# Order of gathers and weight fetches in an expert layer behind block-sparse attention

## The chip, the core and the metric

The kernel runs on one core of a Trainium2 chip. The metric is the device time of one execution in microseconds (us). Five engines work side by side: TensorE (PE) multiplies matrices, VectorE (DVE) and ScalarE (ACT) do elementwise work and empty PE's accumulators, GpSimd (POOL) makes index patterns and here issues the indexed transfers, and SyncE (SP) issues the plain ones. Each engine takes its instructions in the order in which they stand in the program; semaphores hold one back until what it needs is there. A matrix product of f32 operands is two instructions on PE.

## The reference

Block-sparse attention on 4 batches of 8 heads, 768 positions and 64 features, then a layer of 8 experts in which every token goes to the one expert with the highest logit:

```python
scores = scale * np.matmul(q, k.transpose(0, 1, 3, 2))
scores = np.where(mask, scores, -1000000000.0)       # window, first and last blocks, 3 random blocks
scores = scores - np.max(scores, axis=-1, keepdims=True)
attn = np.exp(scores)
attn = attn / (np.sum(attn, axis=-1, keepdims=True) + 1e-09)
attn_out = np.matmul(attn, v)
x = attn_out.transpose(0, 2, 1, 3).reshape(B * S, H * D)     # 3072 tokens x 512
# experts
logits = x @ w_gate                                   # 3072 x 8
expert_idx = np.argmax(logits, axis=1)
gate_w = softmax(logits)[np.arange(N), expert_idx]    # shortened
for e in range(E):                                    # the tokens of expert e
    h = np.maximum(x_sorted[lo:hi] @ w1[e], 0.0)      # w1[e]: 512 x 1024
    y_sorted[lo:hi] = h @ w2[e]                       # w2[e]: 1024 x 512
return gate_w[:, None] * y                            # y put back in token order
```

All is float32. One expert's `w1` and its `w2` have 2048 KB each.

## The kernel before

The first part runs attention in 16 pairs of heads and writes the token rows, with the gate weight at their end, to a scratch tensor `x_d` in device memory. The second part sorts the tokens by expert into tiles of 128 tokens, 28 with these inputs, and for each tile gathers its rows, transposes them, runs both layers and scatters the result into the output. The first five tiles (`KA = 5`) are laid out early, from the first three batches alone, so that their gathers and weights can start during attention (routing table "A"); the others use table "B", which is ready only after attention.

The start. `kT` and `qT` of the first pair are transposed by PE and copied half by VectorE, half by ScalarE:

```python
def turn(b, pr, which, first=None):
    ...
    for half in range(2):
        tp = ps_t.tile(...)[:] if first is None else first[:, half, :CW]
        for c in range(HC):
            nc.tensor.transpose(tp[:, c * P : (c + 1) * P], src[...], ident[:])
        if half == 0:
            nc.vector.tensor_copy(dst[:, :CW], tp)
        else:
            nc.scalar.copy(dst[:, CW:], tp)
        yield
```

Constants for the token layout, called in step 30 of the 96 steps of attention. `sm` is a pool with a place of its own for every tile; `small` has four buffers per tag, which are passed on in turn:

```python
def route_consts():
    iota("first_w", ...); iota("thr", ...); iota("kx", ...); iota("iota_r", ...)
    t1 = sm.tile([P, B, NCH], I32, name="t1")
    nc.gpsimd.iota(t1[:], pattern=[[S, B], [1, NCH]], base=1, channel_multiplier=NCH)
    t2 = sm.tile([P, 2, NT], I32, name="t2")
    flat = t1.rearrange("p b c -> p (b c)")
    nc.vector.tensor_scalar(t2[:, 0, :], flat, scalar1=6, ..., op0=ALU.arith_shift_right)
    nc.vector.tensor_scalar(t2[:, 1, :], flat, scalar1=63, ..., op0=ALU.bitwise_and)
    tok = rt["tok"] = sm.tile([P, 2, NT], BF16, name="tok")
    nc.gpsimd.tensor_copy(tok[:], t2[:])
    ...                                   # lt, all, zero, keep: GpSimd memsets
def rows_out(n, half):                    # end of each half pair of attention
    ...
    lg = small.tile([P, HC, 2, E], F32, name="lg")
```

The parts of a tile. There are four buffers for gathered rows, two each for `w1`, `w2` and the transposed rows:

```python
def gather(i):
    xg = st[i]["xg"] = keep_xg[i % 4]
    nc.gpsimd.indirect_dma_start(out=xg[:], in_=x_d[: N - S, :] if i < KA else x_d[:, :],
                                 in_offset=bass.IndirectOffsetOnAxis(ap=of("g", i, P), axis=0), ...)
def fetch(i, layer):
    e = nc.sync.value_load(of("xe", i, 1), ...)           # the tile's expert
    if layer == 1:
        w = st[i]["w1"] = keep_w1[i % 2];  nc.sync.dma_start(w[:], w1v[:, bass.ds(e, 1)]...)   # L606
    else:
        w = st[i]["w2"] = keep_w2[i % 2];  nc.sync.dma_start(w[:], w2v[:, bass.ds(e, 1)]...)   # L609
def turn_x(i):
    ...                                                   # 4 transposes on PE (L614), one copy
def layer1(i, *between):
    hT = st[i]["hT"] = xp.tile([P, FB, P], F32, name="hT")
    for g in range(2):
        hp = upper["ps_h"].tile(...)
        ...                                               # 16 products into hp (L630)
        ...                                               # relu into hT, VectorE or ScalarE
        if g == 0:
            for do in between:
                do()
def layer2(i, group):
    zp = ps_o.tile([P, DM], F32, name="zp", tag="o")
    ...                                                   # 8 products into zp (L645)
    zo = xp.tile([P, DM], F32, name="zo")
    ...                                                   # zo = zp * gate weight, which lies in xg
    nc.gpsimd.indirect_dma_start(out=out[:, :], ..., in_=zo[:], ...)      # the scatter (L654)
```

The order of the parts. GpSimd and PE keep the order of the program until `by_hand.close()`; the other engines, and those two afterwards, are ordered by a scheduler. The tiles above 24 are in one of the branches of a switch, by how many there are:

```python
            if (n, half) == (NA + 2, 0):                  # in attention, table A
                tokens("A", TA, KA)
                for i_ in range(2):
                    gather(i_)
                    fetch(i_, 1)
                    fetch(i_, 2)
    ...
    layer1(0, lambda: rows_out(*steps[-1][:2]), lambda: turn_x(1))
    for i in range(NT):                                   # NT = 24
        if i == 0:
            ranks("B", TA, NT)
        for t in {1: (3, 4), 2: ()}.get(i, (i + 2,)):
            if t != KA:
                gather(t)
        fetch(i + 2, 1)
        if i + 1 < NT:
            layer1(i + 1, lambda: turn_x(i + 2))
        if i == 0:
            count("B"); layout_b()
        if i == 1:
            tokens("B", NT, NB_)
        layer2(i, "rows_out")
        fetch(i + 2, 2)
        if i == 1:
            gather(KA)
        if i == 2:
            judge()
        if i == KA + 1:
            by_hand.close()
    for extra in tc.Switch(...):
        last = NT + extra
        for i in range(NT, last):
            if i + 2 < last:
                gather(i + 2)
            layer1(i, *([lambda: turn_x(i + 1)] if i + 1 < last else []))
            if i + 2 < last:
                fetch(i + 2, 1)
            layer2(i, "rows_out")
            if i + 2 < last:
                fetch(i + 2, 2)
```

So on PE the first layer of tile i+1 comes ahead of the second layer of tile i, and the transpose of tile i+2 stands in the middle of that first layer. Fetches into a buffer wait until the products that read it are done.

Of the kernel before, what the change touches and what calls it, by code (L numbers as in the profile page):

```python
# [9 lines left out]
I32 = mybir.dt.int32  # L10
# [7 lines left out]
def kernel(  # L18
# [12 lines left out]
    P = 128  # L31
    B, H, S, D = q.shape
# [3 lines left out]
    NCH = S // P  # L36
# [7 lines left out]
    NT = N // P  # L44
    NC = NT + E - 1
    TA = NT - NCH
    KA = 5
# [136 lines left out]
    sm = ctx.enter_context(tc.tile_pool(name="sm", bufs=1))  # L184
    work = ctx.enter_context(tc.tile_pool(name="work", bufs=2))
    small = ctx.enter_context(tc.tile_pool(name="small", bufs=4))
# [199 lines left out]
    def route_consts():  # L386
        iota("first_w", [P, E], [[-1, E]], E, 0)
        iota("thr", [P, NT], [[P, NT]], 0, 0)
        iota("kx", [1, NC], [[1, NC]], 0, 0)
        iota("iota_r", [P, P], [[1, P]], 0, 0)  # L390

        t1 = sm.tile([P, B, NCH], I32, name="t1")
        nc.gpsimd.iota(t1[:], pattern=[[S, B], [1, NCH]], base=1, channel_multiplier=NCH)
        t2 = sm.tile([P, 2, NT], I32, name="t2")
        flat = t1.rearrange("p b c -> p (b c)")
        nc.vector.tensor_scalar(t2[:, 0, :], flat, scalar1=6, scalar2=None, op0=ALU.arith_shift_right)
        nc.vector.tensor_scalar(t2[:, 1, :], flat, scalar1=63, scalar2=None, op0=ALU.bitwise_and)
        tok = rt["tok"] = sm.tile([P, 2, NT], BF16, name="tok")
        nc.gpsimd.tensor_copy(tok[:], t2[:])
        lt = rt["lt"] = sm.tile([P, P], BF16, name="lt")  # L400
        nc.gpsimd.memset(lt[:], 1.0)
        nc.gpsimd.affine_select(
            out=lt[:], in_=lt[:], compare_op=ALU.is_gt, fill=0.0, base=0, pattern=[[1, P]], channel_multiplier=-1,
        )
        rt["all"] = sm.tile([P, P], BF16, name="all_")
        nc.gpsimd.memset(rt["all"][:], 1.0)
        rt["zero"] = sm.tile([P, E], F32, name="zero")
        nc.gpsimd.memset(rt["zero"][:], 0.0)
        keep = rt["keep"] = sm.tile([P, E, TA], F32, name="keep")
        nc.gpsimd.memset(keep[:], 1.0)  # L410
        nc.gpsimd.memset(keep[:, :, 0:1], 0.0)
# [154 lines left out]
    def tokens(ph, T, n):  # L566

        tp = ps_x.tile([P, 2, n], F32, name="tok" + ph, tag="xr")
        for t in range(T):
            nc.tensor.matmul(tp[:], lhsT=rt["or" + ph][:, t, :], rhs=rt["tk" + ph][:, t], start=(t == 0), stop=(t == T - 1))  # L570
        lo = sm.tile([P, n], F32, name="lo" + ph)
        nc.vector.tensor_scalar_add(lo[:], tp[:, 1, :], -1.0)
        tv = sm.tile([P, n], F32, name="tv" + ph)
        nc.vector.scalar_tensor_tensor(tv[:], in0=tp[:, 0, :], scalar=64.0, in1=lo[:], op0=ALU.mult, op1=ALU.add)
        g = rt["g" + ph] = sm.tile([P, n], I32, name="g" + ph)
        nc.vector.tensor_scalar(g[:], tv[:], scalar1=0.0, scalar2=float(T * P - 1), op0=ALU.max, op1=ALU.min)
        none = sm.tile([P, n], F32, name="none" + ph)
        nc.vector.tensor_scalar(none[:], tv[:], scalar1=0.0, scalar2=float(2 * N), op0=ALU.is_lt, op1=ALU.mult)
        s_ = rt["s" + ph] = sm.tile([P, n], I32, name="s" + ph)
        nc.vector.tensor_add(s_[:], tv[:], none[:])  # L580
# [14 lines left out]
    def gather(i):  # L595
        xg = st[i]["xg"] = keep_xg[i % 4]
        nc.gpsimd.indirect_dma_start(  # L597
            out=xg[:], out_offset=None, in_=x_d[: N - S, :] if i < KA else x_d[:, :], in_offset=bass.IndirectOffsetOnAxis(ap=of("g", i, P), axis=0),
        )

    def fetch(i, layer):

        e = nc.sync.value_load(of("xe", i, 1), min_val=0, max_val=E - 1)
        if layer == 1:
            w = st[i]["w1"] = keep_w1[i % 2]
            nc.sync.dma_start(w[:], w1v[:, bass.ds(e, 1)].rearrange("p e c f -> p (e c) f"))  # L606
        else:
            w = st[i]["w2"] = keep_w2[i % 2]
            nc.sync.dma_start(w[:], w2v[:, bass.ds(e, 1)].rearrange("p e a d -> p (e a) d"))  # L609

    def turn_x(i):
        tp = ps_t.tile([P, DB, P], F32, name="tp0", tag="t") if i == 0 else upper["ps_m"].tile([P, DB, P], F32, name="tpg")
        for c in range(DB):
            nc.tensor.transpose(tp[:, c, :], st[i]["xg"][:, c * P : (c + 1) * P], ident[:])  # L614
        st[i]["xT"] = keep_xT[i % 2]

        if i <= KA:
            nc.scalar.copy(st[i]["xT"][:], tp[:])
        else:
            nc.vector.tensor_copy(st[i]["xT"][:], tp[:])  # L620
# [5 lines that stand above are left out]
            hp = upper["ps_h"].tile([P, FB // 2, P], F32, name="hp")  # L626
            for m in range(FB // 2):
                fb = g * (FB // 2) + m
                for c in range(DB):
                    nc.tensor.matmul(  # L630
                        hp[:, m, :], lhsT=st[i]["w1"][:, c, fb * P : (fb + 1) * P], rhs=st[i]["xT"][:, c, :],
                        start=(c == 0), stop=(c == DB - 1),
                    )
            if g == 0 and i >= KA:
                nc.vector.tensor_relu(hT[:, : FB // 2, :], hp[:])  # L635
            else:
                nc.scalar.activation(hT[:, g * (FB // 2) : (g + 1) * (FB // 2), :], hp[:], AF.Relu)  # L637
# [3 lines that stand above are left out]
# [31 lines left out]
    for i in range(len(steps) + 1):  # L672
        at = steps[i] if i < len(steps) else None
        if at is not None:
            n, half, g = at
            if half == 1 and g == 0 and n + 2 < len(pairs):
                load(*pairs[n + 2])
            for c in range(g * GR, (g + 1) * GR):
                scores(n, half, c)
            if i == 1:  # L680
                make_mix()
            if i == 30:
                route_consts()
        if i > 0:
            n, half, g = steps[i - 1]
            for c in range(g * GR, (g + 1) * GR):
                attend(n, half, c)

        if at is not None and at[2] == 1:
            n, half, _ = at  # L690
            turning = turn(*pairs[n + 1], half) if n + 1 < len(pairs) else iter(())
            next(turning, None)
            if i > 3:
                rows_out(*steps[i - 2][:2])
            for _ in turning:
                pass

            if (n, half) == (NA, 0):
                ranks("A", 0, TA)
            if (n, half) == (NA, 1):  # L700
                count("A")
                layout_a()
            if (n, half) == (NA + 2, 0):
                tokens("A", TA, KA)
                for i_ in range(2):
                    gather(i_)
                    fetch(i_, 1)
                    fetch(i_, 2)
            if n + 1 == len(pairs) and half == 1:
                turn_x(0)  # L710
    lend(lent, ps_h=2, ps_m=2)
    layer1(0, lambda: rows_out(*steps[-1][:2]), lambda: turn_x(1))
    for i in range(NT):
        if i == 0:
            ranks("B", TA, NT)
        for t in {1: (3, 4), 2: ()}.get(i, (i + 2,)):
            if t != KA:
                gather(t)
        fetch(i + 2, 1)
        if i + 1 < NT:  # L720
            layer1(i + 1, lambda: turn_x(i + 2))
        if i == 0:
            count("B")
            layout_b()
        if i == 1:
            tokens("B", NT, NB_)
        layer2(i, "rows_out")
        fetch(i + 2, 2)
        if i == 1:
            gather(KA)  # L730
        if i == 2:
            judge()
        if i == KA + 1:
            by_hand.close()

    for extra in tc.Switch(nc.values_load(rt["more"][0:1, 0:1], min_val=0, max_val=NC - NT), NC - NT + 1):
        last = NT + extra
        for i in range(NT, last):
            if i + 2 < last:
                gather(i + 2)  # L740
            layer1(i, *([lambda: turn_x(i + 1)] if i + 1 < last else []))
            if i + 2 < last:
                fetch(i + 2, 1)
# [3 lines that stand above are left out]
# [54 lines left out]
```

## Time and profile before

| | |
|---|---|
| time, median of 3 runs | 904.13 us (900.5 to 904.48) |
| span of the profiled execution | 904.3 us |
| PE busy | 833.7 us, 92% of the span |
| DVE, ACT, POOL busy | 293.9, 214.9, 68.2 us |
| device memory read, written | 143.79 MB, 13.73 MB |
| PE clock, mean | 0.971 of full |

The page first gives each engine's busy time, then the span in 40 slices of about 22.6 us with a digit for the busy tenths, and then groups of like instructions. A row of a group names the line of the kernel, the engine, the operation, the tile written and the tiles read, shape, type and count; after the bar stand busy us and the mean ns of one, and then how long the engine sat idle just ahead of these instructions and what ended most of that. A timeline row has the start, the length, the engine (SPq is SyncE issuing a transfer), the line, and in brackets the idle time before it with what ended it. The name `w` stands for both layers' weights; L630 is the first layer, L645 the second. Attention reaches to about 424 us, the expert part from there to about 890.

### The profile page before, as it was taken

How to read it: one execution, taken by the hardware profiler on the slowest of the kernel's cores; microseconds unless marked ns; L12 is line 12 of the kernel's file. 1: busy time of each engine (PE TensorE's matmuls, PEld its weight loads, DVE VectorE, ACT ScalarE, POOL GpSimd, SP SyncE). 2: the span in 40 equal slices, each digit the busy share in tenths (PEclk: the TensorE clock that was granted, in tenths of full speed). 3: DMA queues.
4: the chain of work that ended last, by engine and by line, in shares of the span. 5: the costliest groups of instructions: out<-in, count | busy, mean ns of one | idle time of the engine just before them, and what ended most of it. 6: DMA issues, size and time to landing. Idle time of an engine off the chain costs nothing.

```text
span 904.3 us, 12472 instructions
## 1 busy us (share of the span) xinstructions
PE 833.7 (92%) x5104; PEld 529.0 (59%) x5104; DVE 293.9 (33%) x613; ACT 214.9 (24%) x306; POOL 68.2 (8%) x102
## 2 busy tenths in 40 slices
PE   6999999999999998999969777998999999999993
PEld 3455545555455554556857555766576766766671
DVE  4455555555555567554600000011111101111110
ACT  2444454444544444443111000000000000000000
POOL 4000000000000000010010001010110101010100
PEclk7999999999999999999989888999999999999997
DMA  7122222212222237410359755579788797879950
GB/s 157 44 64 68 55 71 71 71 42 64 71 53 70 54 72 257 183 39 20 123 214 335 274 194 190 192 277 341 267 308 306 266 353 272 321 272 350 397 180 9
DMA packets 119238, 157.52 MB, mean 174 GB/s; under 512 B 56435, under 2 KB 72819, under 8 KB 119156
## 3 DMA queue, kind: packets, MB, share of 16 engines
q1 hardware_dynamic: 112544, 142.32, 47.3%
q0 software_dynamic: 4480, 13.75, 4.0%
q8 instruction: 44, 0.72, 0.3%
q10 hardware_dynamic: 2132, 0.41, 0.2%
q14 instruction: 38, 0.31, 0.1%
HBM read 143.79 MB, written 13.73 MB: 174 GB/s over the span
## 4 chain that ended last, share of the span: by engine, by line
PE 48%; issue 38%; DMA 7%; POOL 3%; DVE 2%; another core or an unknown queue 0%; ACTq 0%; POOLq 0%; ACT 0%; DVEq 0%
PE s L216 15%; PE op L236 15%; DMA out_dram<-zo,sB 5%; PE xr L252 4%; PE s L219 3%; PE hp L630 3%; PE xr L257 3%; PE tp L197 3%; POOL xg L597 2%; PE zp L645 2%; POOL out_dram L654 1%; DMA xg<-x_rows,gB 1%; DVE esum L227 1%; DMA wg<-in_moe_w_gate_dram 1%; DVE orA L561 0%
## 5 line engine op out<-in xcount | busy, mean ns | idle before, releaser
L630 PE MATMUL hp<-xgT,w 128*128 128x128 f32 x1792 | 218.9, 283 | 16.0 <-DMA w<-in_moe_w_dram 15.9
L630 PEld LDWEIGHTS hp<-xgT,w 128*128 128x128 f32 x1792 | 214.6, 199 | 32.3 <-issue 19.0
L645 PE MATMUL zp<-w,hT 128*128 128x512 f32 x448 | 197.0, 593 | 0.6 <-DVE hT L635 0.6
L221 ACT ACTIVATE e<-s 128x768 f32<-128x768 f32 x192 | 155.8, 813 | 94.2 <-PE s L219 92.3
L216 PE MATMUL s<-qT,kT 64*128 64x384 f32 x768 | 166.9, 513 | 0.0
L227 DVE TENSOR_TENSOR esum<-esum,e 128x768 f32<-128x768 f32 x128 | 122.6, 958 | 69.9 <-ACT e L221 63.2
L236 PE MATMUL op<-e,v_sb 128*64 128x384 f32 x768 | 144.8, 499 | 0.0
L645 PEld LDWEIGHTS zp<-w,hT 128*128 128x128 f32 x448 | 83.0, 190 | 95.0 <-issue 94.2
L637 ACT ACTIVATE hT<-hp 128x512 f32<-128x512 f32 x33 | 19.7, 597 | 389.7 <-PE hp L630 386.8
L216 PEld LDWEIGHTS s<-qT,kT 64*128 64x128 f32 x768 | 63.8, 188 | 64.9 <-ACT e L221 37.6
L236 PEld LDWEIGHTS op<-e,v_sb 128*64 128x64 f32 x768 | 46.7, 136 | 80.1 <-issue 79.9
L653 DVE TENSOR_SCALAR zo<-zp,xg 128x512 f32<-128x512 f32 x23 | 17.3, 751 | 217.8 <-PE zp L645 217.8
L219 PE MATMUL s<-pen,oh 64*128 64x384 bf16 x384 | 63.6, 325 | 0.0
L635 DVE TENSOR_SCALAR hT<-hp 128x512 f32<-128x512 f32 x23 | 15.9, 692 | 118.1 <-PE hp L630 111.4
L227 DVE TENSOR_TENSOR esum<-e 128x768 f32<-128x768 f32 x32 | 30.7, 959 | 64.8 <-ACT e L221 64.8
L654 POOL DMA_INDIRECT out_dram<-zo,sB x23 | 23.2, 1009 | 304.3 <-DVE zo L653 304.3
L252 PEld LDWEIGHTS xr<-ones,esum 128*128 128x128 f32 x384 | 45.4, 192 | 1.2 <-DVE esum L227 1.2
L252 PE MATMUL xr<-ones,esum 128*128 128x1 f32 x384 | 44.9, 244 | 0.0
L614 PE MATMUL tpg<-ident,xg 128*128 128x128 f32 x108 | 18.3, 296 | 26.8 <-DMA xg<-x_rows,gB 19.6
L597 POOL DMA_INDIRECT xg<-x_rows,gA x5 | 6.4, 1284 | 370.1 <-PE s L219 368.9
L219 PEld LDWEIGHTS <-oh 64*128 64x128 bf16 x384 | 19.4, 95 | 25.1 <-issue 0.6
L257 PE MATMUL xr<-mix,oT 128*128 128x144 f32 x192 | 31.4, 300 | 0.0
(185 smaller groups left out, 307.8 us busy)
## 6 DMA issues: line engine op xcount, KB each, us to landing
w<-in_moe_w_dram SPq DMA_DIRECT2D x56, 2048.0 KB, 12.0
k_sb<-in_k_dram SPq DMA_DIRECT2D x32, 192.0 KB, 3.6
v_sb<-in_v_dram SPq DMA_DIRECT2D x16, 384.0 KB, 3.2
x_rows<-xb SPq DMA_DIRECT2D x16, 384.0 KB, 3.8
q_sb<-in_q_dram SPq DMA_DIRECT2D x30, 192.0 KB, 3.3
q_sb<-in_q_dram ACTq DMA_DIRECT2D x2, 192.0 KB, 4.9
xg<-x_rows,gB POOLq DMA_INDIRECT x23, 7.7
out_dram<-zo,sB POOLq DMA_INDIRECT x23, 7.8
```

The costliest lines, as they stand in the source:

```text
L197: nc.tensor.transpose(tp[:, c * P : (c + 1) * P], src[:, half * HC + c].rearrange("p h d -> p (h d)"), ident[:],)
L216: nc.tensor.matmul(s[:, hh, :CW], lhsT=kT[r, c * P : (c + 1) * P], rhs=qT[r, cols], start=True, stop=False)
L219: nc.tensor.matmul(s[:, hh, :CW], lhsT=oh[r, c, :], rhs=pen[r, cols], start=False, stop=True)
L221: nc.scalar.activation(e[:], s[:, :, :CW], AF.Exp, scale=scale)
L227: nc.vector.tensor_add(t[:], es[(n, half, 0)][:] if c == 1 else t[:], e[:])
L236: nc.tensor.matmul(op[hh * D : (hh + 1) * D, :], lhsT=v_sb[:, hh, c, :], rhs=e[:, hh, :], start=(c == 0), stop=(c == NCH - 1),)
L252: nc.tensor.matmul(xr[:, HC * M + 2 * m + hh : HC * M + 2 * m + hh + 1], lhsT=esum[:, hh, m * P : (m + 1) * P], rhs=ones[:], start=True, s ...
L257: nc.tensor.matmul(xr[:, m * M : (m + 1) * M], lhsT=oT[:, m * P : (m + 1) * P], rhs=mix[:, pr, :], start=True, stop=True)
L597: nc.gpsimd.indirect_dma_start(out=xg[:], out_offset=None, in_=x_d[: N - S, :] if i < KA else x_d[:, :], in_offset=bass.IndirectOffsetOnAx ...
L630: nc.tensor.matmul(hp[:, m, :], lhsT=st[i]["w1"][:, c, fb * P : (fb + 1) * P], rhs=st[i]["xT"][:, c, :], start=(c == 0), stop=(c == DB - 1),)
L645: nc.tensor.matmul(zp[:], lhsT=st[i]["hT"][:, fb, :], rhs=st[i]["w2"][:, fb, :], start=(fb == 0), stop=(fb == FB - 1),)
L654: ins = nc.gpsimd.indirect_dma_start(out=out[:, :], out_offset=bass.IndirectOffsetOnAxis(ap=of("s", i, P), axis=0), in_=zo[:], in_offset=N ...
```

## The change

Gathers are issued three tiles ahead of the tile in work instead of two, which the four row buffers allow; three, not two, are issued in attention. The fetch of first-layer weights moves behind the first layer of the tile before last, whose buffer it takes, so that it no longer goes out together with a second-layer fetch. The two integer tiles of the layout constants take buffers of the logit tiles instead of places of their own, which also moves their two VectorE operations to the place in the attention where they are called.

```diff
-        t1 = sm.tile([P, B, NCH], I32, name="t1")
+        t1 = small.tile([P, B, NCH], I32, name="t1", tag="lg")
         nc.gpsimd.iota(t1[:], pattern=[[S, B], [1, NCH]], base=1, channel_multiplier=NCH)
-        t2 = sm.tile([P, 2, NT], I32, name="t2")
+        t2 = small.tile([P, 2, NT], I32, name="t2", tag="lg")
...
                 tokens("A", TA, KA)
+                for i_ in range(3):
+                    gather(i_)
                 for i_ in range(2):
-                    gather(i_)
                     fetch(i_, 1)
                     fetch(i_, 2)
...
     layer1(0, lambda: rows_out(*steps[-1][:2]), lambda: turn_x(1))
+    fetch(2, 1)
     for i in range(NT):
         if i == 0:
             ranks("B", TA, NT)
-        for t in {1: (3, 4), 2: ()}.get(i, (i + 2,)):
-            if t != KA:
-                gather(t)
-        fetch(i + 2, 1)
+        gather(i + 3)
         if i + 1 < NT:
             layer1(i + 1, lambda: turn_x(i + 2))
+            fetch(i + 3, 1)
...
         layer2(i, "rows_out")
         fetch(i + 2, 2)
-        if i == 1:
-            gather(KA)
         if i == 2:
             judge()
...
         for i in range(NT, last):
-            if i + 2 < last:
-                gather(i + 2)
+            if i + 3 < last:
+                gather(i + 3)
```

## Prediction

> **What bounds the kernel now.** I read the page's 40 slices first. TensorE (PE) has digit 9 nearly everywhere, so the attention stage, up to about 424 us, leaves nothing to a change of order. It falls to 6 to 7 in slices 21 to 25, at a reduced clock. The costliest groups name what it waits for:
>
> ```profile
> L630 PE MATMUL hp<-xgT,w 128*128 128x128 f32 x1792 | 218.9, 283 | 16.0 <-DMA w<-in_moe_w_dram 15.9
> L645 PE MATMUL zp<-w,hT 128*128 128x512 f32 x448 | 197.0, 593 | 0.6 <-DVE hT L635 0.6
> L614 PE MATMUL tpg<-ident,xg 128*128 128x128 f32 x108 | 18.3, 296 | 26.8 <-DMA xg<-x_rows,gB 19.6
> ```
>
> The expert stage waits 15.9 us for weights ahead of the first layer and 26.8 us for gathered tokens ahead of the transpose, and never for second-layer weights. The windows of the attention stage, the early expert stage and the late one show what this does to PE busy time (second column), clock, DMA share and GB/s (last three):
>
> ```profile
> 100.00:200.00 100.00, 100.00 (x665) 52.90 (x664) 54.16 (x107) 46.73 (x65) 0.00 (x0) 1.00 0.26 64
> 448.00:592.00 144.00, 114.55 (x616) 85.81 (x615) 13.89 (x24) 10.95 (x18) 15.60 (x15) 0.89 0.65 231
> 592.00:817.00 225.00, 211.68 (x1238) 154.71 (x1239) 29.90 (x45) 8.36 (x14) 29.84 (x30) 1.00 0.83 299
> ```
>
> PE's timeline shows a gather wait, GpSimd's timeline (POOL) why it is there:
>
> ```profile
> 505.50 3.73 PE L630 MATMUL hp<-xgT,w 128*128 128x128 f32 x32
> 515.64 1.12 PE L614 MATMUL tpg<-ident,xg 128*128 128x128 f32 x4 [6.40 <-DMA xg<-x_rows,gB]
> 516.55 5.74 PE L630 MATMUL hp<-xgT,w 128*128 128x128 f32 x32
> 522.13 7.03 PE L645 MATMUL zp<-w,hT 128*128 128x512 f32 x16
> ```
> ```profile
> 506.72 1.01 POOL L654 DMA_INDIRECT out_dram<-zo,sA  x1 [17.32 <-ACT zo L651]
> 508.03 1.00 POOL L597 DMA_INDIRECT xg<-x_rows,gB  x1 [0.30 <-issue]
> ```
>
> GpSimd works in order. The gather of tile 6 stands behind the output scatter of tile 3, which waits for tile 3's second layer (done at 505.5). The transpose wants tile 6 half a first layer later, at 509.1; the gather, issued at 508.03, lands after 7.6 us. The first layer's second half then takes 5.74 us, not the usual 3.74: the clock has dropped. SyncE's timeline shows both weight fetches going out as a pair:
>
> ```profile
> 607.26 0.37 SPq L609 DMA_DIRECT2D w<-in_moe_w_dram  x1
> 607.82 0.45 SPq L606 DMA_DIRECT2D w<-in_moe_w_dram  x1
> ```
>
> The first-layer weights of the pair are needed one tile later, and PE starts on them at 624.66, 16.84 us after the issue.
>
> At the very start VectorE (DVE) waits 4.6 us for a layout constant, with the copy that the scores need queued behind it:
>
> ```profile
> 13.64 0.16 POOL L393 IOTA t<- 128x24 int32 x1
> 13.84 0.18 DVE L396 TENSOR_SCALAR t<-t 128x24 int32<-128x24 int32 x1 [4.64 <-POOL t L393]
> ...
> 14.01 0.55 DVE L201 COPY qT<-first 128x384 f32<-128x384 f32 x1
> ...
> 14.61 0.50 PEld L197 LDWEIGHTS first<-ident,q_sb 128*128 128x128 f32 x3 [4.22 <-DVE qT L201]
> ```
>
> **What the Trainium skill says.** "TensorE: Matmul & The Clock Gate", Part 1, says that an idle window of about 3.4 us halves PE's clock and that it takes about one busy window to restore it. The trace agrees: mean clock 0.89 where the gather waits lie, and 5.74 against 3.74 us above. So a removed wait gives back more than itself. "DMA: Bandwidth & Descriptors", section "Issuing engines are not separate DMA queues", says that transfers from all issuers share the same 16 engines and interleave. The trace agrees: a gather lands after 3.6 us at the least, 7.7 in the median, with the weights beside it. The same page's "Rules for kernel authors" advises issuing a transfer early and waiting for it late, which is what this change does.
>
> **Part 1, gathers three ahead.** An undisturbed tile takes 14.45 us (the first layer starts at 846.74 and the next at 861.19): half a first layer 3.57, transpose 0.43, other half 3.58, second layer 6.87. The four gather waits, with the slow matmuls after them, as the timeline has them against this:
> - tile 3: transpose at 459.61, due at 452.24, so 7.37; transpose and half layer take 5.54 for 4.01, so 1.53 more. Sum 8.90.
> - tile 6: 6.57 + 2.48 = 9.05. Tile 7: 6.69 + 2.61 = 9.30. Tile 8: 6.85 + 2.60 = 9.45.
>
> Together 36.7 us. In the new GpSimd order the gather of tile 3 goes out with tiles 0 to 2, near 389 us, into a fourth buffer nobody has used. Each later gather, of tile i+3, stands behind the scatter of tile i-1, about 2.5 us after that tile's second layer ends. Its transpose is then one first layer (7.58), one second layer (6.87) and half a first layer (3.57) away: 18.0 us, or 15.5 after the issue. The longest gather of the trace took 8.9. The gathers cost the same; they add nothing to PE. I count all 36.7. From tile 9 on, the old kernel's scheduler already had its gathers this far ahead (two follow each other at 555.34 and 556.63), so nothing more is to be had there.
>
> **Part 2, first-layer fetches behind the first layer.** The weight waits: between the first-layer starts at 576.65 and 810.14 lie 15 tiles, 233.49 us, against 15 x 14.45 = 216.75, so 16.74. One more at 487.3: 2.08 of waiting and a half layer of 5.27 for 3.57, so 3.78. Together 20.5. Now w1 of tile i+3 is issued when the first layer of tile i+1 ends, instead of after the second layer of tile i. It is due two second layers and a first one later: 6.87 + 7.58 + 6.87 = 21.3 us, against some 13.9 before. The slowest weight fetch took 16.7 us as half of a pair, one alone 8.3. The second-layer fetch keeps its place and its 22.0 us.
>
> Throughput allows it: two fetches of 2048 KB (4.19 MB), a gather (128 x 520 x 4 = 0.27) and a scatter (0.26) are 4.72 MB in 14.45 us, 327 GB/s. The steady stage above averages 299, but only because the DMA stands idle between pairs; where it is full it moves more:
>
> ```profile
> 601.30:602.30 1.00, 1.00 (x3) 0.38 (x2) 0.00 (x0) 0.00 (x0) 0.00 (x0) 1.00 1.01 412
> 606.30:607.30 1.00, 1.00 (x4) 0.28 (x3) 0.03 (x1) 0.00 (x0) 0.00 (x0) 1.00 0.01 4
> 831.40:861.20 29.80, 29.23 (x170) 21.33 (x169) 4.08 (x6) 1.20 (x2) 3.99 (x4) 1.00 1.04 401
> ```
>
> The last row is the tail, whose code already fetches in the alternating way: 401 GB/s and PE busy for 29.23 of 29.80 us. I count all 20.5.
>
> **Part 3, constants late.** Moved into the rotating buffers of the logit tiles, the two VectorE operations leave the start and stand after about a third of the attention. The copy of qT could then begin when PE has done its transposes, 9.94 + 0.85 = 10.79, instead of 14.01: 3.2 us, all on the path, since PE is busy from there on. PE runs at half clock around there; if the rise to full clock doesn't move along, only half of the 3.2 stays. Later VectorE waits once for GpSimd's following constants, about 1.4 us (GpSimd's row from tok to keep in the start), while it is idle nearly half the time; I charge 0.5.
>
> **Sum.** 36.7 + 20.5 + 3.2 - 0.5 = 59.9 us; 904.1 - 59.9 = 844.2. I predict 844 us. Not touched: the 0.57 us wait at the entry of the tail, and the 14.5 us from PE's last second layer (889.7) to the end.
>
> **Rivals.**
> - *The DMA becomes the bound.* If the streams sustained only the 299 GB/s of the steady stage, a tile would take 4.72 / 299 = 15.8 us and part 2 would vanish, perhaps with new waits for second-layer weights: about 865. Against it stand 401 GB/s in the tail and the idle microseconds between pairs.
> - *The gather stays late behind the scatter.* It is still behind it in GpSimd's queue. If it missed its transpose again, part 1 would shrink to tile 3: about 872. Against it: 15.5 us of room for 8.9.
> - *A new wait in order.* SyncE now interleaves 1 to 3 loads of expert numbers (about 0.57 us each) with the fetches, and gathers 5 and up need the second routing table. VectorE finishes that table's inputs at 453.28, 11.4 us after its counts at 441.91; PE now comes to it after 14.6. Were it late, a few us are lost once: about 847.
>
> **Range and chances.** The first two rivals I give about 5% each, partial forms included. The runs before spread by 4 us, the start is good for 1.6 to 3.5, and small waits I don't see may keep 3 to 6 us. The range is 839 to 852. Faster by over 2% (under 886) 0.97, within 2% 0.025, slower 0.005.
>
> **What would show it.** Right: no PE wait for xg; waits for w before L630 near zero; first layers every 14.45 us through the whole stage; granted clock 1.00 after about 19 us; GB/s steady near 327 in the late expert stage; the first scores near 12.3 us instead of 15.44; PE ending near 830. Wrong: a wait for w before L645, a period near 15.8, or an xg wait still behind the scatter.

## The result, and the profile after

| | before | changed |
|---|---|---|
| time, median of 4 runs each | 904.31 us | 845.94 us (845.3 to 846.65) |
| span of the profiled execution | 904.3 us | 844.9 us |
| PE busy, share of the span | 833.7 us, 92% | 820.4 us, 97% |
| mean PE clock | 0.971 | 0.993 |

The changed kernel takes 0.936 of the time before, 95% interval 0.933 to 0.939. Predicted were 844 us, with a range of 839 to 852.

The mean clock of the changed kernel is a little too high: its record has no half clock from 0 to 20 us, although the products there run at half speed until 17.4 us (four score products take 1.49 us at 16.02 and 0.81 at 17.51). For the start, the lengths of the products are the better measure.

The rows of the page's group list for the first and the second layer, in the changed kernel:

```profile
L630 PE MATMUL hp<-xgT,w 128*128 128x128 f32 x1792 | 209.1, 275 | 0.0
L645 PE MATMUL zp<-w,hT 128*128 128x512 f32 x448 | 197.0, 593 | 0.9 <-DVE hT L635 0.9
```

Ahead of the first layer 16.0 us of waiting have become 0.0, and the mean of one product has gone from 283 to 275 ns, because the clock no longer falls in this stage (1.00 in the windows below). The transpose has left the page's list; the view of its tile shows all 108 products between 272 and 273 ns and no idle time of PE:

```profile
L614 PE MATMUL tpg<-ident,xg x108: 272/273/273, 427.6 to 806.0; 128*128 128x128 f32 x108
```

The windows of the expert stage (PE busy in the second column; clock, DMA share and GB/s at the end) show PE busy for every microsecond of them:

```profile
443.00:580.00 137.00, 137.00 (x815) 100.34 (x814) 20.03 (x42) 12.04 (x20) 20.19 (x20) 1.00 0.90 320
580.00:770.00 190.00, 190.00 (x1082) 137.63 (x1081) 26.53 (x39) 7.76 (x13) 26.77 (x27) 1.00 0.92 325
```

Why the gather is no longer late is seen when GpSimd's timeline is laid beside PE's:

```profile
506.27 1.02 POOL L654 DMA_INDIRECT out_dram<-zo,sA  x1 [12.15 <-ACT zo L651]
507.59 0.98 POOL L597 DMA_INDIRECT xg<-x_rows,gB  x1 [0.30 <-issue]
```
```profile
505.05 3.73 PE L630 MATMUL hp<-xgT,w 128*128 128x128 f32 x32
508.62 0.60 PE L614 MATMUL tpg<-ident,xg 128*128 128x128 f32 x4
509.06 3.74 PE L630 MATMUL hp<-xgT,w 128*128 128x128 f32 x32
512.63 7.03 PE L645 MATMUL zp<-w,hT 128*128 128x512 f32 x16
519.50 3.73 PE L630 MATMUL hp<-xgT,w 128*128 128x128 f32 x32
523.07 0.60 PE L614 MATMUL tpg<-ident,xg 128*128 128x128 f32 x4
```

The gather still stands right behind a scatter and goes out 2.5 us after a second layer has ended (505.05). But it is for the transpose at 523.07, not for the one at 508.62, and has 15.5 us. First layers follow each other at 14.45 us (505.05, 519.50). SyncE's timeline no longer has pairs; L609 fetches second-layer weights, L606 first-layer ones:

```profile
606.39 0.37 SPq L609 DMA_DIRECT2D w<-in_moe_w_dram  x1
613.98 0.37 SPq L606 DMA_DIRECT2D w<-in_moe_w_dram  x1
```

The view of the weight tiles gives 7.9, 9.7 and 13.3 us from issue to landing (least, median, most), against 8.3, 12.0 and 16.7 before. At the start, VectorE waits for nothing but PE's transposes before it copies qT, at 11.21 instead of 14.01 us:

```profile
10.33 0.85 PE L197 MATMUL first<-ident,q_sb 128*128 128x128 f32 x3
...
11.21 0.56 DVE L201 COPY qT<-first 128x384 f32<-128x384 f32 x1 [1.64 <-PE first L197]
...
11.83 0.90 PE L197 MATMUL first<-ident,q_sb 128*128 128x128 f32 x3 [0.65 <-DVE qT L201]
...
12.66 1.65 PE L216 MATMUL s<-qT,kT 64*128 64x384 f32 x4
```

The first scores start at 12.66 instead of 15.44 us.

### The profile page after: what moved, and what is told of

Its sections match the earlier page's. It is cut to its first block, busy times and chain, and to the rows that moved or that the text cites. A ratio compares the mean times of both kernels' runs of the same rounds, so it can differ in the third digit from the quotient of the medians.

```text
span 844.9 us, 12494 instructions
## 1 busy us (share of the span) xinstructions
PE 820.4 (97%) x5104; PEld 519.8 (62%) x5104; DVE 293.4 (35%) x613; ACT 214.6 (25%) x306; POOL 69.3 (8%) x102
## 4 chain that ended last, share of the span: by engine, by line
issue 44%; PE 42%; DMA 5%; POOL 4%; DVE 3%; another core or an unknown queue 0%; POOLq 0%; ACT 0%; DVEq 0%
PE s L216 15%; PE op L236 14%; DMA out_dram<-zo,sB 5%; PE xr L252 4%; PE s L219 3%; POOL xg L597 3%; PE xr L257 3%; PE tp L197 3%; POOL out_dram L654 1%; DVE esum L227 1%; PE first L197 0%; DVE allow L151 0%; DVE orA L561 0%; DVE kT L201 0%
## 5 line engine op out<-in xcount | busy, mean ns | idle before, releaser
L630 PEld LDWEIGHTS hp<-xgT,w 128*128 128x128 f32 x1792 | 206.3, 192 | 12.6 <-issue 12.6
L630 PE MATMUL hp<-xgT,w 128*128 128x128 f32 x1792 | 209.1, 275 | 0.0
L645 PE MATMUL zp<-w,hT 128*128 128x512 f32 x448 | 197.0, 593 | 0.9 <-DVE hT L635 0.9
L645 PEld LDWEIGHTS zp<-w,hT 128*128 128x128 f32 x448 | 83.1, 190 | 95.3 <-issue 94.2
L257 PEld LDWEIGHTS xr<-mix,oT 128*128 128x128 f32 x192 | 25.4, 191 | 0.0
```

Of the source, the lines that this page charges most:

```text
L257: nc.tensor.matmul(xr[:, m * M : (m + 1) * M], lhsT=oT[:, m * P : (m + 1) * P], rhs=mix[:, pr, :], start=True, stop=True)
L630: nc.tensor.matmul(hp[:, m, :], lhsT=st[i]["w1"][:, c, fb * P : (fb + 1) * P], rhs=st[i]["xT"][:, c, :], start=(c == 0), stop=(c == DB - 1),)
L645: nc.tensor.matmul(zp[:], lhsT=st[i]["hT"][:, fb, :], rhs=st[i]["w2"][:, fb, :], start=(fb == 0), stop=(fb == FB - 1),)
```

## The experiments

The theory: three separate waits of PE have been removed. The gather was due before it could land, the first-layer fetch was held in SyncE's queue behind a second-layer fetch, and the start waited for a constant. The main rivals: the DMA engines are the bound or nearly so; the gathers were late because paired weights crowded them. `before` and `changed` below name the kernel that was edited.

### Part 1 alone

```diff
 before
+                for i_ in range(3):
+                    gather(i_)
                 for i_ in range(2):
-                    gather(i_)
...
-        for t in {1: (3, 4), 2: ()}.get(i, (i + 2,)):
-            if t != KA:
-                gather(t)
+        gather(i + 3)
         fetch(i + 2, 1)
...
-        if i == 1:
-            gather(KA)
...
-            if i + 2 < last:
-                gather(i + 2)
+            if i + 3 < last:
+                gather(i + 3)
```

> Part 1 alone (gathers three ahead; fetches and constants as before). Theory: the four gather waits and their slow matmuls (36.7 us) go. But while PE stood in them, the paired weight fetches had time to land; without them the weight waits, 16.74 us over 15 tiles or 1.12 us a tile, appear on the early tiles too: about 23 tiles x 1.12 = 25.7 us instead of 20.5. So 904.3 - 36.7 + 5.2 = 873 us, waits for w ahead of L630 over 20 us, none for xg. Rival A, the parts simply add: 868. Rival B, the gather stays late because it is still behind the scatter: over 885, with xg waits left.

Measured: 874.6 us, ratio 0.966 (0.961 to 0.970). No wait for xg is left. In the group list the waits ahead of the first layer are now longer than in the kernel before, 19.3 us against 16.0 and a little under the 20 expected:

```profile
L630 PE MATMUL hp<-xgT,w 128*128 128x128 f32 x1792 | 213.6, 278 | 19.3 <-DMA w<-in_moe_w_dram 15.7 <-DVE zo L653 3.6
```

I count the 3.6 us put down to zo as waits for weights too: in the changed kernel the same products stand in the same place and never wait for zo. PE's timeline shows it on the early tiles, where the gather waits used to be:

```profile
499.14 3.81 PE L630 MATMUL hp<-xgT,w 128*128 128x128 f32 x32 [1.50 <-DMA w<-in_moe_w_dram]
514.40 3.81 PE L630 MATMUL hp<-xgT,w 128*128 128x128 f32 x32 [0.58 <-DMA w<-in_moe_w_dram]
```

What follows: the parts don't simply add. The interval of the ratio is 870 to 878 us; the theory's 873 lies in it, the 868 of rival A just outside, and the uncovered waits in the trace tell against rival A as well. A wait that is removed uncovers another one that it had hidden, and part 1 alone is worth 30.4 us (905.0 - 874.6).

### Part 2 alone

```diff
 before
     layer1(0, lambda: rows_out(*steps[-1][:2]), lambda: turn_x(1))
+    fetch(2, 1)
...
-        fetch(i + 2, 1)
         if i + 1 < NT:
             layer1(i + 1, lambda: turn_x(i + 2))
+            fetch(i + 3, 1)
```

> Part 2 alone (first-layer fetches behind the first layer; gathers and constants as before). Theory: the weight waits (20.5 us) go, the four gather waits of 6.4 to 7.2 us stay, since the gather's place in GpSimd's queue is unchanged: 904.3 - 20.5 = 884 us, xg waits about 27 us. Rival, the gathers land late because both fetches of a pair fill the DMA engines just then: with the pair split the gather lands some 2 to 4 us sooner, xg waits fall to 11 to 19 us, time 865 to 875.

Measured: 886.4 us, ratio 0.980 (0.975 to 0.985). The two rows of the group list:

```profile
L630 PE MATMUL hp<-xgT,w 128*128 128x128 f32 x1792 | 216.7, 281 | 0.0
L614 PE MATMUL tpg<-ident,xg 128*128 128x128 f32 x108 | 18.3, 296 | 26.0 <-DMA xg<-x_rows,gB 19.3 <-DMA xg<-x_rows,gA 6.6
```

The weight waits are gone; the gather waits are 26.0 us, against 26.8 before, and a gather lands after 7.6 us in the median, against 7.7. The rival falls: splitting the pair hardly makes a gather land sooner. It was issued too late: from 508.03 on, even the quickest gather of the trace before (3.6 us) would have landed at 511.6, and the transpose was due at 509.1. How much of the other 4 us is owed to the one second-layer fetch that goes out some 2 us ahead of the gather, no run here separates.

### Part 3 alone

```diff
 before
-        t1 = sm.tile([P, B, NCH], I32, name="t1")
+        t1 = small.tile([P, B, NCH], I32, name="t1", tag="lg")
...
-        t2 = sm.tile([P, 2, NT], I32, name="t2")
+        t2 = small.tile([P, 2, NT], I32, name="t2", tag="lg")
```

> Part 3 alone (constants late). Theory: the first scores start about 2.8 us earlier and the whole attention moves with them: 904.3 - 2.5 = 901.8 us, expert stage unchanged. Rival, the start is hidden by the wait for data or given back when VectorE waits for the late constants: 904 us.

Measured: 901.5 us, ratio 0.9956 (0.9934 to 0.9978), so 3.5 us, between 2 and 6. In its trace the first scores start at 12.25 us instead of 15.44 and the first expert layer at 420.75 instead of 424.32:

```profile
12.25 1.65 PE L216 MATMUL s<-qT,kT 64*128 64x384 f32 x4
...
420.75 3.84 PE L630 MATMUL hp<-xgT,w 128*128 128x128 f32 x32
```

The gain reaches the end, and the rival (904) falls.

### The pair the other way round

```diff
 changed
             layer1(i + 1, lambda: turn_x(i + 2))
             fetch(i + 3, 1)
+            if i > 0:
+                fetch(i + 1, 2)
...
         layer2(i, "rows_out")
-        fetch(i + 2, 2)
+        if i + 1 >= NT:
+            fetch(i + 1, 2)
+            fetch(i + 2, 2)
```

> The changed kernel with the pair put back the other way round: the second-layer weights of tile i+1 go out together with, and behind, the first-layer weights of tile i+3, one first layer later than now. Same bytes, same number of fetches. Theory: what cost time was a fetch that stands second in a pair and is due some 14 us later; now that is w2, so waits for w come back ahead of L645 (none ahead of L630), 1 to 2 us a tile over some 21 tiles: 862 to 885 us, with some clock loss at most. Rival, only the early issue of w1 mattered and the DMA engines have room for pairs: 846 us.

Measured: 869.1 us, ratio to before 0.958 (0.953 to 0.964). SyncE's timeline shows the pair, PE's the second layer that waits for its second half:

```profile
633.23 0.37 SPq L606 DMA_DIRECT2D w<-in_moe_w_dram  x1
633.79 0.37 SPq L609 DMA_DIRECT2D w<-in_moe_w_dram  x1
```
```profile
649.93 8.83 PE L645 MATMUL zp<-w,hT 128*128 128x512 f32 x16 [2.28 <-DMA w<-in_moe_w_dram]
...
785.76 9.78 PE L645 MATMUL zp<-w,hT 128*128 128x512 f32 x16 [7.50 <-DMA w<-in_moe_w_dram]
```

The waits have moved from the first to the second layer (15.4 us ahead of L645, none ahead of L630), with the same bytes, as the theory says; the rival (846) falls. The edit also leaves a second-layer fetch less time, some 14 us instead of 22, but in the changed kernel none took more than 13.3 us to land; here, in the pair, the slowest took 16.1. The size needs care. The last row is the end of the loop, where two second layers follow each other and the fetch has only half as long: due at 778.1, it starts at 785.76 and takes 9.6 instead of 6.9, together 10.4 us that belong to this edit's end. That leaves 868.0 - 844.9 - 10.4 = 12.7 us, 0.6 us a tile rather than the 1 to 2 expected. With runs from 864.3 to 869.7 us, the 12.7 are rough.

### Written behind the second layer, but ahead of the other fetch

```diff
 changed
             layer1(i + 1, lambda: turn_x(i + 2))
-            fetch(i + 3, 1)
...
         layer2(i, "rows_out")
+        if i + 1 < NT:
+            fetch(i + 3, 1)
         fetch(i + 2, 2)
```

> The changed kernel with the fetch of first-layer weights put back behind the second layer in the program, but written one line ahead of the second-layer fetch instead of one behind it. Theory: the old wait was one of SyncE's queue; w1's buffer had been free since the first layer ended, and its fetch only stood behind a w2 fetch that waits for the second layer. Ahead of it, w1 goes out at the end of the first layer all the same: 846 us, no waits for w ahead of L630. Rival: the place after the second layer is what delays it, so that the pair stays and lands as late as before (due after 14 us, the second of a pair up to 17): about 865 us with some 20 us of waits for w.

Measured: 846.2 us, ratio to before 0.938 (0.933 to 0.942), as the changed kernel. No wait for w is left ahead of L630. SyncE's timeline has the two fetches 7.6 us apart again, the second of them right at the end of a first layer (599.26):

```profile
591.87 0.37 SPq L609 DMA_DIRECT2D w<-in_moe_w_dram  x1
599.45 0.37 SPq L606 DMA_DIRECT2D w<-in_moe_w_dram  x1
```

The whole of part 2 is one change of places in SyncE's queue. The fetch waits for its buffer alone, as long as nothing with a later condition stands ahead of it. What no run separates is whether the first-layer weights now come in time because their fetch is no longer second in a pair, or because it goes out some 21 us ahead of its use instead of 14. By the landing times either might do: 13.3 us at most without pairs, 16.7 with them.

### More bytes

```diff
 changed
+    spare = wp.tile([P, 4, DM], F32, name="spare")       # 8 instead of 4 for 2 MB
...
             w = st[i]["w2"] = keep_w2[i % 2]
             nc.sync.dma_start(w[:], w2v[:, bass.ds(e, 1)]...)
+            if 2 <= i < NT + 2:
+                nc.sync.dma_start(spare[:], w2v[:, bass.ds(e, 1), :4]...)
```

> The changed kernel with 1 MB more to read per tile: half of the second-layer weights once more into a spare buffer that nothing reads, for 24 tiles. 4.72 + 1.05 = 5.77 MB a tile. Theory (the DMA engines can hold about 402 GB/s, the change needs 327): 5.77 / 402 = 14.35 us, just inside the tile's 14.45, so few waits: 846 to 852 us. Rival (they can hold hardly more than the 325 GB/s that they move now, PE and DMA being balanced): 5.77 / 325 = 17.8 us a tile, over 910 us.

> The changed kernel with 2 MB more per tile (all second-layer weights twice), 6.82 MB. Theory: now the DMA is the bound, 6.82 / 402 = 17.0 us a tile, 24 tiles x 2.5 = 60 us more, less some head start: 895 to 910 us, DMA share about 1.0 throughout. If the rival were right: 6.82 / 325 = 21 us a tile, over 990 us.

Measured: 845.7 us with 1 MB more (ratio to before 0.936, 0.933 to 0.939), 909.4 us with 2 MB more (1.006, 1.004 to 1.008). The windows of the expert stage, first with 1 MB:

```profile
580.00:770.00 190.00, 190.00 (x1079) 136.80 (x1078) 25.93 (x38) 7.76 (x13) 26.44 (x27) 1.00 1.04 396
```

and with 2 MB more:

```profile
580.00:800.00 220.00, 195.29 (x1104) 143.28 (x1105) 26.52 (x39) 7.76 (x13) 27.13 (x28) 0.97 1.03 389
```

1 MB more costs nothing: the engines move 396 GB/s instead of 325, and PE stays busy throughout. With 2 MB they move no more than that, and PE waits. Both times are as the theory had them, within the spread. So the DMA bound for these transfers lies near 390 to 400 GB/s, a fifth above what the changed kernel asks for; the rival is settled.

### A warmer start

```diff
 changed
-        for c in range(14):
+        for c in range(24):
             nc.tensor.transpose(idle[:, 0, :P], ident[:], ident[:])
```

> The changed kernel with 24 instead of 14 idle transposes on PE at the very start, which fill the wait for the mask up to about 7 us, so that PE reaches full clock before the first scores rather than at 17.4 us. Theory: the products from 7.3 to 17.4 us run at full clock, and the scores' start follows from copies as well: 1.5 to 3 us less than the changed kernel, 843 to 844.5 us. Rival: the clock falls again in the waits for the copies (0.6 to 0.7 us each), or the longer filling delays the mask product: 846 us or a little more.

Measured: 845.6 us, ratio to before 0.936 (0.933 to 0.939): no difference from the changed kernel (845.9) that could be told from the spread. The theory, 1.5 to 3 us, falls; in the traces the expert stage starts at 421.13 instead of 421.88, so a gain of under 1 us may be there. The windows of its start (clock in the third column from the right) show full clock from 5.7 us and half clock again from 9.2:

```profile
5.70:9.20 3.50, 1.63 (x11) 0.83 (x9) 3.00 (x6) 0.00 (x0) 1.91 (x4) 0.99 1.25 255
9.20:12.60 3.40, 2.73 (x11) 2.00 (x13) 0.56 (x1) 0.73 (x2) 2.72 (x16) 0.50 1.20 275
12.60:16.00 3.40, 3.40 (x14) 1.78 (x14) 0.00 (x0) 1.18 (x3) 0.65 (x3) 0.50 1.28 257
```

In the window of 3.5 us before the fall PE was busy for only 1.63. Whether filling those waits too would hold the clock was not tried.

## Why the prediction was right, step by step

- **Gathers, 36.7 us.** Right in mechanism, and in size when it is the last part added: from part 2 alone to the changed kernel there are 886.4 - 845.9 = 40.5 us, of which part 3's 3.5, so 37.0. That this comes within 0.3 us is luck, since the four runs of part 2 alone spread by 5.5. Added first, it is worth 30.4. The room of 15.5 us was what the trace then showed.
- **First-layer fetches, 20.5 us.** Right for the sum, because both kinds of wait stood in the trace and both went. But it is not the worth of this part by itself: alone it gives 905.0 - 886.4 = 18.6, and on top of the others 874.6 - 845.9 - 3.5 = 25.2. The prediction didn't say that the gather waits hid weight waits; it needed no such term only because it removed both.
- **The two together, 57.2 us.** From the first expert layer to PE's last product there were 889.7 - 424.3 = 465.4 us; now it is 830.6 - 421.9 = 408.7. That is 56.7. The wait at the entry of the tail, which I left as it was, has grown from 0.57 to 0.91 us.
- **Constants, 3.2 - 0.5 us.** The first scores come 2.78 us earlier and the expert stage 2.44. The 0.34 between go with the clock, as far as the traces tell: it rose at 19.0 us before and at 17.4 now, so 4.7 instead of 3.6 us of scores ran at half clock, which by my estimate costs about 0.6. In the run of part 3 alone it rose at 14.9 us, and there the gain grew on the way, from 3.19 us at the first scores to 3.57 at the expert stage. VectorE's later wait is there (1.26 us, I had said 1.4), and no wait of PE comes from it; the 0.5 charged for it was not needed.
- **Throughput.** 327 GB/s were worked out, 325 measured. The first rival, DMA as the bound, was judged by idle microseconds between pairs and by the tail's 401 GB/s; the runs with more bytes, at up to 396 GB/s, bear this out. The third rival, a late second routing table, did not come: PE reaches its products at 453.81 without a wait.
- **The signs named.** No wait for xg, none for w ahead of L630, 14.45 us from first layer to first layer, PE's end at 830.6 (said: near 830): all came. The first scores at 12.66 were a little later than the 12.3 said: the mask product ran at half clock this time (0.82 us against 0.49). One reading was loose without consequence: of the slices 21 to 25 the 22nd shows 9, not 6 to 7.

The sum of the three parts run singly is 30.4 + 18.6 + 3.5 = 52.5 us; together they give 58 to 59. The 6 us between are about what part 1 alone falls short of its 36.7, the weight waits that it uncovers.

## What to carry to other kernels

Ask of every late transfer what it stands behind in its issuing engine's queue, and for which later step its buffer really has to be there: both large gains here came from a place in a queue, with the same bytes and the same buffers. Read the DMA's limit from where it is full, not from its mean, because engines that idle between bursts look less than full (0.83 here) and still deliver late. Count waits for removal together, not one by one: the early tiles showed no weight wait only because they stood waiting for something else.

## What had not been expected of the hardware

Short waits can cost the clock. The Trainium skill, "TensorE: Matmul & The Clock Gate", Part 1, speaks of an idle window of about 3.4 us. In the kernel before, a wait of 1.89 us was followed by half a first layer of 5.44 us instead of 3.74; in the run of part 1 alone waits of 2.21 and 2.95 us were followed by 5.44 as well. Yet waits of 2.83 and 2.78 us in the kernel before were followed by 3.81. The page calls the window free-running, so where the wait falls in it may decide; no run here was made to show that.

A gather of 128 rows needs 7.6 us in the median even where weight fetches are spread out (3.5 to 8.7 in the changed kernel), about as long as beside pairs (7.7). Where it goes out some 9 us behind a pair, in the run with the pair the other way round, the median is 5.7.
